# A single-core attention and mixer kernel: even query weights, mixer steps of 5, 5 and 4, and a part of one step's keys on GpSimd's queue

## The chip, the cores and the metric

The kernel runs on one core of a Trainium2 chip. The core has a matrix engine (TensorE, PE in the profile), a vector engine (VectorE, DVE), a scalar engine (ScalarE, ACT), a general one (GpSimd, POOL) and a sync engine (SyncE, SP) that here does nothing but ask for transfers. Sixteen DMA engines move data between the chip's memory and the core's on-chip memory of 128 partitions. The metric is the time of one execution in microseconds (us), lower is better; the time before is the median of 3 runs.

## The reference, cut to what matters

One decode step (one new token for each of 8 sequences) of a block in which attention and a token mixer stand side by side:

```python
# x (8, 1, 512); k_cache, v_cache (8, 8, 8192, 128); wq (512, 4096); wo (4096, 512); F = 1792
xn = layernorm(x)
q = (xn @ wq) as (8 rows, 32 heads, 1, 128)         # 4 query heads share one head of keys
p = softmax(q @ k.T * 128 ** -0.5)                  # over 8192 cached positions
A = (p @ v) as (8, 1, 4096) @ wo
h = layernorm(xn)                                   # (8, 1, 512)
B = gelu(h^T * w1 + b1) @ w2 + b2                   # per batch row: 512 channels, 1792 hidden units
out = x + A + B
```

All is float32. Keys and values are 8 x 8 x 8192 x 128 x 4 bytes = 268 MB each, wq and wo 8.4 MB each; all of it has to be read once.

## The kernel before, in words

The work runs in 32 steps (`duo_step(i)`, i from 0 to 31). A step is one pair of key-value heads of one batch row; its keys and its values are 8 MB each (128 partitions x 64 KB: partition p holds 128 consecutive positions of one of the two heads). They lie in a ring of five slots of 4 MB (`slots`, tile `raw`). A step's keys take two slots and its values two.

In a step, DVE transposes the keys in place, 32 x 32 blocks at a time (L347), in two halves of four instructions; PE multiplies each piece with the queries (L357) into `acc`. After the first half of a step's scores SP may ask for the next step's keys, since the slots that these go to were read by then (`load_next()` at L478). Then comes the maximum (L370), its spread over partitions (L375, L377), the exponential on ACT (L383), a matmul and a transpose that bring the weights into place (L389, L390), and the product with the values of the step before (L398), after whose second half SP asks for the next values (L499). The order in which SP asks is the list `plan`; the order of every engine's instructions is the order of the calls in the code.

Every four steps of a group, `place_duo` (L408 to L428) divides and folds the results. The mixer runs beside it in small steps: `mix(n)` (L455, called at L510 with n = 4) takes the next n of 8 x 14 mixer steps. A mixer step is a GELU on ACT (L443) and a multiplication and an addition on POOL (L444, L445) into `macc`. When a batch row's 14 steps are over, the first mixer step of the next row begins with `mx_end` (PE sums `macc` over partitions, L449, and DVE adds the row to `yrow`, L450) and `mx_begin` (PE L435, POOL L437). With four steps a call, a row of 14 ends inside a call for every second row, and at the start of one for the others.

At the start, wq is loaded in two manners. 448 of its 512 rows go evenly over the partitions, in two loads of 128 x 7168 numbers, into the slots 2 and 3 (`body`, L85, L128). The other 64 rows go into slot 4 (`extra`) by small loads from SP and POOL (L100 to L124), each of which brings a chosen number of rows to chosen DMA engines; tiny loads on POOL (`pass_over`, L111) move the choice of engine on. By the sizes of these loads eight engines receive 4 to 11 rows of 16 KB each and the other eight none. PE multiplies them (L317) in the order of arrival: first and second half of `body`, then `extra`. A DMA of a few rows is spread over the engines row by row; a load over all 128 partitions gives every engine the same.

PE's instructions are themselves fetched by DMA while the program runs: 36 transfers of 16 KB (queue q8 of the profile), which in this trace fall on eight of the sixteen engines in turn, those that get no extra rows of wq.

## Time and profile before

| | us |
|---|---|
| median of 3 runs (1290.19 to 1291.01) | 1290.56 |
| profiled execution | 1292.12 |
| its span, first to last instruction | 1290.4 |
| PE busy with matmuls | 769.5 |
| DVE busy | 685.7 |
| POOL busy | 234.9 |
| ACT busy | 221.2 |
| data moved: 554.39 MB, mean rate | 430 GB/s |
| mean granted TensorE clock | 0.808 of full speed |

The prediction quotes rows of the profile. Rows of DMA queues read: queue, kind, packets, megabytes, share of the time of 16 engines. Rows of the chain read: start (us from the span's start), length, what; the chain goes back from the last instruction to whatever released each piece. Rows of a timeline read: start, busy us, engine, line, operation, output and input tile, shape, and in brackets how long the engine had been idle and what ended that. "L347" is line 347 of the kernel before.

### The profile page before, as it was taken

The numbers are of one execution on the slowest core, as the hardware profiler recorded it, in microseconds if no ns is written. First come the engines' busy times: TensorE is split into PE (matmuls) and PEld (weight loads), VectorE is DVE, ScalarE is ACT, GpSimd is POOL, SyncE is SP. The second block draws the span as 40 slices with busy tenths as digits, with TensorE's granted clock in tenths as the row PEclk, the third lists the DMA queues.
The fourth block names the chain that finished last, engine by engine and source line by source line (L and its number), as shares of the span: only waits on it lengthen the run. The fifth ranks groups of instructions, "written<-read, shape, count | busy, mean of one in ns | idle before, by whom it ended". The sixth has DMA issues, their size and how long they took to land.

```text
span 1290.4 us, 10900 instructions
## 1 busy us (share of the span) xinstructions
PE 769.5 (60%) x4656; PEld 162.6 (13%) x4656; DVE 685.7 (53%) x567; ACT 221.2 (17%) x321; POOL 234.9 (18%) x254
## 2 busy tenths in 40 slices
PE   3665565765556675465565665576456764456676
PEld 1210011110111110011110111111011110011112
DVE  5745544565644465544465554466544565544561
ACT  1030222121221111222121222102222121200000
POOL 3031222022221112222112222102222012200000
PEclk8896777887778877888887787887777877778879
DMA  9999999999999999999999999999999999999998
GB/s 385 434 441 433 433 429 431 440 425 437 435 429 439 429 435 431 433 438 431 434 435 429 431 429 433 427 437 437 429 437 431 431 436 433 435 431 431 441 421 344
DMA packets 12067, 554.39 MB, mean 430 GB/s; under 512 B 1941, under 2 KB 1973, under 8 KB 2369
## 3 DMA queue, kind: packets, MB, share of 16 engines
q1 hardware_dynamic: 11316, 553.08, 99.2%
q8 instruction: 36, 0.59, 0.2%
q0 software_dynamic: 672, 0.61, 0.1%
q14 instruction: 11, 0.09, 0.0%
q10 hardware_dynamic: 32, 0.02, 0.0%
HBM read 553.69 MB, written 0.02 MB: 429 GB/s over the span
## 4 chain that ended last, share of the span: by engine, by line
DMA 71%; DVE 21%; PE 7%; ACT 1%; issue 0%; SPq 0%; POOL 0%; ACTq 0%; DVEq 0%
DMA raw<-in_A_k_cache_dram 60%; DVE raw L347 21%; DMA raw<-in_A_v_cache_dram 7%; PE acc L357 3%; PE acc L398 3%; DMA raw<-in_A_wo_dram 2%; DMA raw<-in_A_wq_dram 1%; PE misc L317 0%; PE misc L422 0%; POOL macc L445 0%; ACT raw L91 0%; PE misc L389 0%; PE misc L449 0%; SPq L187 0%; ACT g L443 0%
## 5 line engine op out<-in xcount | busy, mean ns | idle before, releaser
L347 DVE STREAM_TRANSPOSE raw<-raw 128x2048 f32<-128x2048 f32 x256 | 565.3, 2274 | 215.7 <-DMA raw<-in_A_k_cache_dram 215.7
L357 PE MATMUL acc<-raw,z 128*32 128x512 f32 x2048 | 377.8, 823 | 448.1 <-DVE raw L347 445.7
L398 PE MATMUL acc<-raw,pt 128*32 128x512 f32 x2048 | 242.7, 616 | 7.5 <-DMA raw<-in_A_v_cache_dram 6.9
L444 POOL TENSOR_SCALAR g<-g,pad 128x512 f32<-128x512 f32 x112 | 77.4, 691 | 759.0 <-ACT g L443 759.0
L357 PEld LDWEIGHTS acc<-raw,z 128*32 128x32 f32 x2048 | 47.2, 124 | 763.1 <-DVE raw L347 486.5
L445 POOL TENSOR_TENSOR macc<-macc,g 128x512 f32<-128x512 f32 x112 | 141.6, 1265 | 9.3
L383 ACT ACTIVATE t2k<-acc,nb 128x512 f32<-128x512 f32 x32 | 22.0, 687 | 651.9 <-DVE nb L377 651.9
L443 ACT ACTIVATE g<-hb,pad 128x512 f32<-128x512 f32 x112 | 87.0, 777 | 200.4 <-POOL macc L445 173.5
L390 DVE STREAM_TRANSPOSE pt<-misc 128x512 f32<-128x512 f32 x64 | 45.9, 717 | 139.2 <-PE misc L389 134.7
L398 PEld LDWEIGHTS acc<-raw,pt 128*32 128x32 f32 x2048 | 65.2, 114 | 171.7 <-issue 144.8
L377 DVE CUSTOM_DVE_ANT_0 t2k<-misc,hmask 128x128 f32<-128x128 f32 x32 | 9.3, 292 | 114.5 <-PE misc L375 114.5
L389 PE MATMUL misc<-t2k,send 128*128 128x512 f32 x128 | 63.5, 618 | 2.7 <-ACT t2k L383 2.7
L370 DVE TENSOR_REDUCE mr<-acc 128x1 f32<-128x512 f32 x32 | 22.1, 690 | 51.9 <-PE acc L357 51.9
L406 ACT COPY ob<-acc 128x512 f32<-128x512 f32 x32 | 18.7, 585 | 118.1 <-PE misc L422 55.1
L443 ACT ACT_TABLE_LOAD x28 | 35.9, 1283 | 4.6 <-PE hb L435 4.2
L511 ACT ACT_TABLE_LOAD x28 | 35.9, 1283 | 0.5
L422 PE MATMUL misc<-ob,pick 128*32 128x512 f32 (+2 forms) x72 | 29.0, 546 | 0.7 <-ACT ob L406 0.7
L389 PEld LDWEIGHTS misc<-t2k,send 128*128 128x128 f32 x128 | 21.7, 189 | 44.1 <-issue 41.3
L317 PE MATMUL misc<-raw,ob 128*32 128x512 f32 x88 | 16.9, 890 | 17.2 <-DMA raw<-in_A_wq_dram 17.2
L449 PE MATMUL misc<-macc,bsel 128*8 128x512 f32 x16 | 11.6, 817 | 25.8 <-POOL macc L445 25.8
L450 DVE TENSOR_TENSOR yrow<-misc,yrow 8x512 f32<-8x512 f32 x8 | 5.4, 679 | 30.3 <-PE misc L449 30.3
L437 POOL MEMSET macc<- 128x512 f32 x8 | 4.2, 526 | 89.4 <-PE misc L449 59.7
(91 smaller groups left out, 150.3 us busy)
## 6 DMA issues: line engine op xcount, KB each, us to landing
raw<-in_A_v_cache_dram SPq DMA_DIRECT2D x4, 4096.0 KB
raw<-in_A_k_cache_dram SPq DMA_DIRECT2D x4, 2048.0 KB, 18.2
raw<-in_A_k_cache_dram SPq DMA_DIRECT2D x2, 4096.0 KB
raw<-in_A_wq_dram SPq DMA_DIRECT2D x2, 3584.0 KB, 13.3
raw<-in_A_wo_dram SPq DMA_DIRECT2D x1, 4096.0 KB
raw<-in_A_wo_dram SPq DMA_DIRECT2D x1, 2048.0 KB
raw<-in_A_wo_dram SPq DMA_DIRECT2D x1, 1024.0 KB, 31.1
raw<-in_A_wo_dram SPq DMA_DIRECT2D x1, 512.0 KB
```

Of the source, the lines that this page charges most:

```text
L347: nc.vector.transpose(t, t)
L357: nc.tensor.matmul(SD[i][c * W:(c + 1) * W, :].rearrange("p (t j) -> p t j", j=W), Z[:, q, b, (1 - k) * REP:(1 - k) * REP + W], t[:, c * C ...
L370: nc.vector.tensor_reduce(mr, SD[i], AX.X, ALU.max)
L383: nc.scalar.activation(p, SD.pop(i), AF.Exp, bias=nb, scale=SCALE, accum_out=LD[e][:, o:o + 1])
L389: nc.tensor.matmul(m, send[:, k, :], p, start=True, stop=True)
L390: nc.vector.transpose(PT[k][:, :CH_T * W], m)
L398: nc.tensor.matmul(OD[i][j * W:(j + 1) * W, :].rearrange("p (c d) -> p c d", c=NCH), PT[k][:, t * W:(t + 1) * W], v[:, t], start=(not k an ...
L422: nc.tensor.matmul(mv, pick[:, c, :], ob[:, :n, c * DH:(c + 1) * DH], start=(c == 0), stop=(c == NCH - 1))
L443: nc.scalar.activation(g, hb, AF.Gelu_apprx_tanh, bias=b1t[:, j:j + 1], scale=w1t[:, j:j + 1])
L444: nc.gpsimd.tensor_scalar(g, g, w2t[:, j:j + 1], 1.0, op0=ALU.mult, op1=ALU.mult)
L445: nc.gpsimd.tensor_add(acc, acc, g)
L511: nc.scalar.activation(small.tile([P, 1], F32, name="warm"), nil, AF.Exp)
```

## The change

The 512 rows of wq go evenly over the partitions, 4 rows to each, in two loads of 4 MB, and the query product takes them in that order; the extra rows, the tiny loads at the start, the tiles and copies that served them go. Keys 0 are asked for in two pieces, keys 1 in one. The mixer takes 5, 5 and 4 steps in turn and starts at step 1, so that each row of 14 ends with a call. And of step 14's keys, SP loads partitions 0 to 111 whole and of partitions 112 to 127 the last 1024 of each 8192 numbers; POOL's queue loads the first 7168 of each 8192 there, in four loads of 2, 6, 2 and 6 partitions, ahead of each a tiny load that moves the choice of engine on. By these sizes, each of eight engines receives 2 partitions x 56 KB = 112 KB from POOL's queue, and each of the sixteen 456 KB from SP's.

```diff
-WJ = 14
...
+MIX = (5, 5, 4)
+MID = 14
+EVEN = P - 16
+APART = 7168
+QE = D // P
+QN = HQ * DH
...
-    nc.sync.dma_start(body[:, :half], rows[:, :half])
...
-    load_block(nc.sync, 0, 5, REP, D0, 6)
-    load_steps(nc.sync, W, REP, 3, D0 + 4, 6)
...
-    nc.sync.dma_start(body[:, half:WJ * WB], rows[:, half:])
-    def load_side():
-        pass_over(7)
-        load_block(nc.gpsimd, 60, 2, REP, D0 + 30, 10, 2)
...
+    rows = wq.rearrange("(p e) n -> p (e n)", p=P)
+    for a in range(2):
+        half = slice(a * QE * QN // 2, (a + 1) * QE * QN // 2)
+        nc.sync.dma_start(body[:, half], rows[:, half])
...
-    plan = [(kc, KP, 0, (k,), (k,), x) for k in range(2) for x in halves]
-    plan += [(kc, KP, 1, (2 + k,), (k,), whole) for k in range(2)]
+    plan = [(kc, KP, 0, (k,), (k,), whole) for k in range(2)]
+    plan.append((kc, KP, 1, (2, 3), (0, 1), None))
...
+    def pass_over(n):
+        at = len(passed) * 4
+        passed.append(n)
+        nc.gpsimd.dma_start(junk[:n, at:at + 3:2].unsqueeze(2), wq[:n, 0:3:2].unsqueeze(2))
+
+    def load_uneven(t, rows):
+        nc.sync.dma_start(t[:EVEN], rows[:EVEN])
+        nc.sync.dma_start(t[EVEN:, :, APART:], rows[EVEN:, :, APART:])
+        at = EVEN
+        for skip, n in ((7, 2), (6, 6), (2, 2), (6, 6)):
+            pass_over(skip)
+            nc.gpsimd.dma_start(t[at:at + n, :, :APART], rows[at:at + n, :, :APART])
+            at += n
...
-        if x is None:
+        if to is KP and i == MID:
+            load_uneven(t.rearrange("p (s m) -> p s m", s=2), rows.rearrange("p (s m) -> p s m", s=2))
+        elif x is None:
             nc.sync.dma_start(t, rows)
...
+        for e in range(QE):
+            for h in range(HKV):
+                g = h % NB
+                nc.tensor.matmul(ms[h // NB][g * W:(g + 1) * W, :], lx[:, e, :],
+                                 body[:, e * QN + h * REP * DH:e * QN + (h + 1) * REP * DH],
+                                 start=(e == 0), stop=(e == QE - 1))
+        load_next()
+        load_next()
...
-        mix(4)
+        if i:
+            mix(MIX[(i - 1) % len(MIX)])
```

On SP's queue the start of the program read, before (`raw` is the ring; each row gives the line, the operation, the output and the input, and the shape):

```order
L85 DMA raw<-in_A_wq_dram 128x7168
L100 DMA raw<-in_A_wq_dram 20x1x4096
L105 DMA raw<-in_A_wq_dram 3x8192
L105 DMA raw<-in_A_wq_dram 2x4096
L120 DMA raw<-in_A_wq_dram 3x2x16
L124 DMA raw<-in_A_wq_dram 2x2x16
L128 DMA raw<-in_A_wq_dram 128x7168
L175 DMA raw<-in_A_k_cache_dram 128x4096 x4
L175 DMA raw<-in_A_k_cache_dram 128x8192 x2
L175 DMA raw<-in_A_v_cache_dram 128x8192 x2
```

and with the change:

```order
L83 DMA raw<-in_A_wq_dram 128x8192 x2
L133 DMA raw<-in_A_k_cache_dram 128x8192 x2
L131 DMA raw<-in_A_k_cache_dram 128x16384
L133 DMA raw<-in_A_v_cache_dram 128x8192 x2
L131 DMA raw<-in_A_k_cache_dram 128x16384
```

The five extra loads of wq on SP are gone, and keys 0 and 1 come in three loads instead of six.

On POOL's queue, between the mixer steps that belong to step 12 and those of step 13, the changed program has (`junk` takes the tiny loads):

```order
L370 TENSOR_SCALAR g<-g,pad 128x512
L371 TENSOR_TENSOR macc<-macc,g 128x512
L110 DMA junk<-in_A_wq_dram 7x2x1
L118 DMA raw<-in_A_k_cache_dram 2x2x7168
L110 DMA junk<-in_A_wq_dram 6x2x1
L118 DMA raw<-in_A_k_cache_dram 6x2x7168
L110 DMA junk<-in_A_wq_dram 2x2x1
L118 DMA raw<-in_A_k_cache_dram 2x2x7168
L110 DMA junk<-in_A_wq_dram 6x2x1
L118 DMA raw<-in_A_k_cache_dram 6x2x7168
L363 MEMSET macc 128x512
```

Before, no load stood there: the clearing of `macc` or the next mixer step followed directly.

On PE, the end of the mixer's fifth row stood before inside the call of step 17 (the rows from step 17's second half of values on; L449 is `mx_end`, L435 `mx_begin`):

```order
L398 MATMUL acc<-raw,pt_246 32x512 x16
L389 MATMUL misc<-t2k,send 128x512 x2
L416 MATMUL misc<-lr_1767,ohg 32x4
L422 MATMUL misc<-ob,pick 32x512 x4
L449 MATMUL misc<-macc,bsel 8x512
L435 MATMUL hb<-hn,ident 128x512
L357 MATMUL acc<-raw,z 32x512 x32
```

and stands now at the start of step 16's call, ahead of all mixer steps of that call (L375 is now `mx_end`, L361 `mx_begin`):

```order
L324 MATMUL acc<-raw,pt_165 32x512 x16
L315 MATMUL misc<-t2k,send 128x512 x2
L375 MATMUL misc<-macc,bsel 8x512
L361 MATMUL hb<-hn,ident 128x512
L283 MATMUL acc<-raw,z 32x512 x32
```

In both programs PE has the row's sum right behind the step's other work and ahead of the next step's scores (L357, now L283); what differs is whether mixer steps of the same call stand ahead of it on ACT and POOL: two of them before, none now.

## The prediction

> **What bounds the kernel now.** I read the page first: the queues (its part 3: packets, megabytes, share of the sixteen DMA engines' time) and the chain that ended last (part 4).

> ```profile
> q1 hardware_dynamic: 11316, 553.08, 99.2%
> q8 instruction: 36, 0.59, 0.2%
> DMA raw<-in_A_k_cache_dram 60%; DVE raw L347 21%; DMA raw<-in_A_v_cache_dram 7%; PE acc L357 3%; PE acc L398 3%; DMA raw<-in_A_wo_dram 2%; DMA raw<-in_A_wq_dram 1%; PE misc L317 0%; PE misc L422 0%; POOL macc L445 0%; ACT raw L91 0%; PE misc L389 0%; PE misc L449 0%; SPq L187 0%; ACT g L443 0%
> ```

> SP's queue keeps the sixteen engines busy for 99.2% of the span, at 553.08 MB / (0.992 x 16 x 1290.4 us) = 27.0 GB/s each. The compute lines in the chain are only the way back to a request for keys: while DVE transposes, the queue still holds other loads. Then I read the chain in order of time (start, length, what).

> ```profile
> 8.17 18.68 DMA raw<-in_A_wq_dram
> 67.50 38.13 DMA raw<-in_A_k_cache_dram
> 105.65 8.90 DVE raw L347 x4
> ...
> 183.00 8.90 DVE raw L347 x4
> ...
> 530.72 8.90 DVE raw L347 x4
> 539.66 1.11 PE acc L357 x8
> 540.79 28.48 DMA raw<-in_A_k_cache_dram
> ...
> 729.16 8.81 DVE raw L347 x4
> 738.01 1.11 PE acc L357 x8
> 739.14 23.37 DMA raw<-in_A_k_cache_dram
> 762.60 8.90 DVE raw L347 x4
> ...
> 1228.49 17.67 DVE raw L347 x8
> ```

> DVE's transposes begin as soon as the last of the sixteen engines has delivered a step's keys, so their starts are landing times of the slowest engine. Keys 2 landed at 105.65, keys 4 at 183.00, keys 13 at 530.72, keys 19 at 762.60, keys 31 at 1228.49. From 4 to 13 a step takes 347.72 / 9 = 38.64 us for 16.78 MB: 434 GB/s, 27.1 GB/s for each engine, 19.32 us for a load of 8 MB. From 19 to 31 it takes 465.89 / 12 = 38.82 us, 2.26 us more in all than at the earlier pace. The time is the load of the slowest engine, and which engine that is changes on the way.

> The extra 2.26 us fit the fetches of PE's instructions. There are 36 of 0.59 MB / 36 = 16 KB, one in about 36 us, shared by eight engines: in 466 us 12.9 of them, 1.6 to an engine, so 1.4 us each if the slowest engine is one that fetches. The page's 0.2% (0.15 to 0.25) of 16 x 1290.4 us over 36 gives 0.86 to 1.43 us. I take 1.4. Before 730 us the pace holds no fetch, so there the slowest engine is one of those that carry the uneven rows of wq. Those rows are these (size in KB, median us from issue to landing):

> ```profile
> raw<-in_A_wq_dram SPq DMA_DIRECT2D x2, 3584.0 KB, 13.3
> raw<-in_A_wq_dram SPq DMA_DIRECT2D x1, 320.0 KB
> raw<-in_A_wq_dram POOLq DMA_DIRECT2D x1, 256.0 KB, 13.2
> raw<-in_A_wq_dram POOLq DMA_DIRECT2D x3, 64.0 KB, 23.1
> ```

> wq's even part is 448 KB to an engine, 16.9 us, yet its last byte lands at 8.17 + 18.68 = 26.85. The engines with many extra rows are some 7 us late from then on.

> **The change, part by part.** *Even wq.* By the landing of keys 2 every engine now moves five loads of 512 KB (wq, keys 0 and 1, values 0, keys 2): 5 x 19.32 = 96.6 us. The start loses time besides (stretch, busy times of the engines, PE's clock, DMA share, GB/s):

> ```profile
> 0.00:12.00 12.00, 0.99 (x6) 0.83 (x6) 8.52 (x56) 5.18 (x4) 8.21 (x16) 1.00 0.88 341
> 12.00:24.00 12.00, 5.19 (x28) 1.30 (x28) 9.94 (x50) 0.29 (x1) 1.13 (x2) 1.00 0.98 409
> 24.00:40.00 16.00, 5.96 (x32) 1.44 (x36) 1.93 (x1) 0.00 (x0) 2.80 (x5) 0.72 1.00 422
> ```

> Against 434 GB/s the first 12 us lose 2.6 us and the next 28 us 1.1 us. The first loss stays; the second, where engines wait between pieces of unequal length, may stay or go (0 to 1.1; I keep it whole, since no row shows the start without the pieces). One fetch for the engine that is now slowest, 1.4. Sum: 96.6 + 2.6 + 1.1 + 1.4 = 101.7 instead of 105.65: **-3.9** (-5.0 with the second loss gone). Five extra loads of wq on SP, twelve on POOL, three of the pieces in which keys 0 and 1 were asked for, and the memsets and copies that scattered x go too; they lie beside the load and are worth nothing. PE's matmuls for q fall from 44 to 32; the last 16 of before (two records each) took

> ```profile
> 39.72 6.08 PE L317 MATMUL misc<-raw,ob 128*32 128x512 f32 x32 [7.16 <-DMA raw<-in_A_wq_dram]
> ```

> so the 16 that now stand behind wq's second half, which lands at about 22 us, end by 28; keys 1 are requested then, while keys 0 keep the engines busy until 41.

> *The fetches from then on.* The fetching engines are no longer ahead; they are the slowest all the way. Five fetches fall on the unluckiest of the eight (36 = 4 x 8 + 4), four of them after keys 2: 4 x 1.4 = 5.6 us on top of 29 x 38.64 = 1120.6 us.

> *Step 14's keys.* SP loads 112 rows whole and, of the last 16, only the last 1024 of each 8192 numbers: 7 x 64 KB + 8 KB = 456 KB to an engine instead of 512 KB, -56 KB or **-2.1**. POOL's queue brings 16 x 56 KB = 896 KB, 112 KB to each of eight engines, 4.2 us each. Those eight have no fetches, so by keys 31 they stand at 4.2 against 7.0 and are not last: nothing on the path. The eight POOL issues (four are tiny loads that only move the choice of engines on) cost 0.6 us each,

> ```profile
> 7.93 0.58 POOL L105 DMA_DIRECT2D raw<-in_A_wq_dram  x1
> q0 software_dynamic: 662, 0.61, 4.4%
> ```

> 4.6 us. POOL has nothing else to do then, by its old timeline (start, length, what, idle before):

> ```profile
> 531.35 1.27 POOL L445 TENSOR_TENSOR macc<-macc,g 128x512 f32<-128x512 f32 x1
> ...
> 565.96 0.69 POOL L444 TENSOR_SCALAR g<-g,pad 128x512 f32<-128x512 f32 x1 [33.34 <-ACT g L443]
> ```

> Step 12's mixing is over at 532.6 and step 13's begins 25 us after the request at 540.79. The first of POOL's four data loads waits, as SP's does, for the first half of step 13's scores; queued behind it on POOL are its next mixing steps alone, and for those ACT waits. Without that cover they would slip by at most the 4.6 us. What rows that go through POOL cost the engines shows only at the start (the second row, for 0 to 40 us): 4.4% of 16 x 40 us is 28 us for 0.61 MB in 662 packets, against 22.5 us by size, so large packets run at the common 27 GB/s. That row is the nearest and I take 4.2 us from it. It does not bound the cost from above: those rows were placed apart for the purpose, these 16 lie side by side. From above I take that the 16 rows get only the pace of the two engines that write them today: 896 KB / 54.3 GB/s = 16.9 us, 12.7 us more.

> Keys 2 to 31 then take 1120.6 + 5.6 - 2.1 = 1124.1 us instead of 1122.84: **+1.3**.

> *Mixer steps 5, 5, 4.* Old step 17 closes a batch row inside a call of four, and PE and DVE stand behind POOL:

> ```profile
> 726.57 1.87 PE L449 MATMUL misc<-macc,bsel 128*8 128x512 f32 x2 [7.90 <-POOL macc L445]
> 728.48 0.68 DVE L450 TENSOR_TENSOR yrow<-misc,yrow 8x512 f32<-8x512 f32 x1 [7.64 <-PE misc L449]
> ```

> Keys 18 had landed by about 723.9 (530.72 + 5 x 38.64), the transposes began at 729.16, so keys 19 were requested 5.3 us late (739.14). The usual lead of a request over the last engine is 28.48 - 19.32 = 9.2 us, here 23.37 - 19.32 = 4.05: enough for the slowest engine, not for those ahead, which gave up their lead. Now every batch row closes at the start of a call, with POOL long done. The slowest engine gains nothing at once; that the fetching engines keep their lead is already in the +1.3, which charges them for no idle time. The five-step calls take one step more of ACT and POOL,

> ```profile
> 720.67 0.79 ACT g L443
> ...
> 723.61 0.79 ACT g L443
> ```

> 2.94 us (723.61 - 720.67), and lie where four-step calls left 33.34 us of POOL idle (above): hidden. If that cover went, one step's excess would delay a request by up to 3 us, still within 9.2.

> *The end.* From keys 31 to the end the program is the same: 61.9 us, and 0.

> The sum is -3.9 + 1.3 = **-2.6 us**. The profiled execution took 1292.12 us around its span of 1290.4, the median of the runs is 1290.56; 1290.56 - 2.6 = **1288.0 us**. Apart from the POOL rows the bounds are -3.7 (start's loss gone) and 0 (a fetch at 1.4 with some idle time left to the engines that fetch).

> [...]

> **The rivals.** *The rows crowd.* The pace belongs to the destination, not to the engine: the eight engines queue up before rows that two engines serve today, and everything behind them in their queues waits. They get up to 12.7 us more, of which the 7.0 - 4.2 = 2.8 us by which they were ahead is free: +9.9, so 1288.0 + 9.9 = 1298. It decides once the detour costs an engine more than 7.0 us instead of 4.2, and the result is slower by over 0.2% from 12.1 (7.0 and the 5.1 from 1288.0 to the bound of 1293.1 below). For it: nothing in this trace had two engines write to the same rows' neighbourhood, so nothing excludes it. Against it: the 28 us for 0.61 MB above. [...]

> *The rows come late.* POOL's loads landed up to 23.1 us after issue (above); the last is issued some 5 us after the request, so all may land 28 us after it, as the old load did (28.48). A few us later, and keys 15 are requested later; 9.2 us of lead absorb that, and engines that are ahead lose at most their lead. 1288 to 1291, say 1290.

> *The rows go to other engines.* The tiny loads are to steer the choice; if it stands elsewhere, fetching engines get the 4.2 us: 1288.0 + 4.2 = 1292, just inside no change.

> *More than forecast.* The start's second loss goes and the fetches cost 1.2: -1.1 - 1.0, 1286.

> **How the numbers follow.** A measurement here can tell 0.2%, 2.6 us, from no change: under 1288.0 is faster, over 1293.1 slower. Forecast as summed 0.45, its own range 1286.9 to 1290.5; rows crowd 0.30 (1291 to 1306, a fifth of it within 0.2%); rows late 0.10; other engines 0.08; more than forecast 0.07. The forecast lies on the line between faster and no change and I halve it. Faster: 0.22 + 0.07 = 0.29. No change: 0.23, 0.06 of the crowding, 0.07 of the late rows and 0.05 of the other engines, 0.41. Slower: 0.24, 0.03 and 0.03, 0.30. The range must hold 8 in 10: 1286.5 to 1300.

> **What would show it.** Keys 2 landing at 101.7 and not 105.65; steps of 38.64 us with 1.4 us more where the slowest engine fetched; about 2 us gained at step 14; no DVE wait on PE misc for yrow over 1 us; keys 31 at 1226. Crowding would show as keys 14 or values 13 landing 5 to 15 us behind the pace, and as POOL's packets far slower than 27 GB/s. I am wrong in mechanism if the steps before 14 are slower than 38.8, or if keys 2 land at 105 as before.

## The result, and the profile after

| | us |
|---|---|
| before, median of 5 runs on the same chip | 1291.01 (1290.19 to 1291.21) |
| changed, median of 5 runs | 1331.98 (1330.25 to 1332.48) |
| ratio, with its 95% interval | 1.0315 (1.0302 to 1.0328) |
| span of the changed kernel's profiled execution | 1330.2 |

The change made the kernel 41.0 us slower, where the prediction said 2.6 us faster and left at most 1300 in its range.

The loss can be seen on the page at once. These are the moved gigabytes per second in 40 equal slices of the span, first before (32.3 us a slice) and then of the changed kernel (33.3 us a slice), and behind them the changed kernel's two queues that carry the load:

```profile
GB/s 385 434 441 433 433 429 431 440 425 437 435 429 439 429 435 431 433 438 431 434 435 429 431 429 433 427 437 437 429 437 431 431 436 433 435 431 431 441 421 344
GB/s 407 429 435 434 434 438 427 438 428 435 430 436 432 436 426 436 297 214 288 415 442 436 432 428 434 434 434 432 428 438 430 432 432 440 424 432 439 434 421 333
q1 hardware_dynamic: 10868, 552.75, 98.4%
q0 software_dynamic: 416, 0.94, 0.4%
```

Slices 17 to 19 of the changed kernel, from 532 to 632 us, run at 297, 214 and 288 GB/s; ahead of them and behind them the stream keeps its old pace. It is the stretch in which step 14's keys come. GpSimd's queue (q0) held the engines for 0.4% of 16 x 1330.2 us, some 85 us (74 to 96 by the rounding), for 0.94 MB that would take 35 us at 27.1 GB/s.

The chain of waits in order of time says what stood there (start, length, what):

```profile
101.69 8.90 DVE raw L273 x4
...
529.24 8.90 DVE raw L273 x4
...
540.74 41.39 DMA raw<-in_A_k_cache_dram
...
582.18 10.40 another core or an unknown queue
...
592.66 19.68 another core or an unknown queue
...
612.41 8.90 DVE raw L273 x4
...
622.49 21.96 DMA raw<-in_A_k_cache_dram
...
644.54 8.90 DVE raw L273 x4
```

Keys 2 landed at 101.69 (the prediction said 101.7) and keys 13 at 529.24. These are SP's first request for keys 14 and the last of GpSimd's four (start, length, what):

```profile
539.31 0.34 SPq L113 DMA_DIRECT2D raw<-in_A_k_cache_dram  x1
543.00 0.58 POOL L118 DMA_DIRECT2D raw<-in_A_k_cache_dram  x1
```

Keys 14 had landed whole at 612.41, 73.1 us after SP's request, where the old one took 28.48. The two pieces of "an unknown queue" are waits whose releaser the trace doesn't name; they lie where GpSimd's rows were still coming (the slowest of its four loads took 69.3 us). From keys 13 to keys 15 the changed kernel took 644.54 - 529.24 = 115.3 us, before 2 x 38.64 = 77.3: 38.0 us more, nearly all of the loss.

The stretch in pieces (stretch, busy times of the engines with their instructions, PE's clock, DMA share, GB/s):

```profile
546.00:580.00 34.00, 17.89 (x91) 4.51 (x91) 6.24 (x11) 5.64 (x8) 6.37 (x7) 0.71 0.96 199
584.00:592.00 8.00, 0.00 (x0) 0.00 (x0) 0.00 (x0) 0.56 (x2) 1.19 (x1) 0.50 0.98 143
594.00:608.00 14.00, 0.00 (x0) 0.00 (x0) 0.00 (x0) 0.00 (x0) 0.00 (x0) 0.50 1.00 277
614.00:622.00 8.00, 5.45 (x32) 0.75 (x32) 8.00 (x5) 0.00 (x0) 0.00 (x0) 0.72 0.21 90
626.00:640.00 14.00, 13.48 (x91) 2.98 (x84) 5.07 (x5) 1.27 (x3) 0.00 (x0) 0.78 1.04 449
```

The last two columns are what matter. From 546 to 580 all sixteen engines are busy (share 0.96) and move 199 GB/s: none waits for work, each piece takes twice as long (the median of those of 64 KB 4.85 us, where it is 2.42 from 626 to 640). It gets worse from 584 to 592 (143 GB/s), when the rest of the keys and values 13, which SP asks for next, are on the queues together. From 614 to 622 the share falls to 0.21: now there is nothing to move, because keys 15 are asked for only after keys 14 have come, at 622.49.

GpSimd's loads in that stretch (size, median us from issue to landing):

```profile
raw<-in_A_k_cache_dram POOLq DMA_DIRECT2D x2, 336.0 KB, 55.4
raw<-in_A_k_cache_dram POOLq DMA_DIRECT2D x2, 112.0 KB, 35.6
```

The prediction expected them to cost the engines 4.2 us each and to land with the rest.

### The profile page after: what moved, and what is told of

It reads as the page before. It is cut to its first block, busy times and chain, and to the rows that moved or that the text cites. A ratio compares the mean times of both kernels' runs of the same rounds, so it can differ in the third digit from the quotient of the medians.

```text
span 1330.2 us, 10766 instructions
## 1 busy us (share of the span) xinstructions
PE 747.7 (56%) x4630; PEld 161.3 (12%) x4630; DVE 677.8 (51%) x509; ACT 206.9 (16%) x311; POOL 230.5 (17%) x249
## 4 chain that ended last, share of the span: by engine, by line
DMA 72%; DVE 21%; PE 4%; another core or an unknown queue 2%; issue 0%; SPq 0%; POOL 0%; DVEq 0%
DMA raw<-in_A_k_cache_dram 66%; DVE raw L273 21%; PE acc L283 3%; DMA raw<-in_A_wo_dram 2%; DMA raw<-in_A_v_cache_dram 2%; DMA raw<-in_A_wq_dram 2%; PE acc L324 1%; PE misc L243 0%; SPq L145 0%; POOL raw L118 0%; PE misc L301 0%; POOL junk L110 0%; DVEq L273 0%; PE hb L460 0%
## 5 line engine op out<-in xcount | busy, mean ns | idle before, releaser
L283 PE MATMUL acc<-raw,z 128*32 128x512 f32 x2048 | 369.4, 806 | 521.3 <-DVE raw L273 508.9
L283 PEld LDWEIGHTS acc<-raw,z 128*32 128x32 f32 x2048 | 47.1, 123 | 829.7 <-DVE raw L273 492.9
L350 DVE TENSOR_TENSOR t2k<-misc,keep 32x512 f32<-32x512 f32 (+2 forms) x9 | 5.7, 629 | 22.6 <-PE misc L348 22.6
L243 PE MATMUL misc<-raw,ob 128*32 128x512 f32 x64 | 9.3, 732 | 12.3 <-DMA raw<-in_A_wq_dram 12.3
L262 PE MATMUL misc<-qt,rep 128*64 128x32 f32 x64 | 3.0, 243 | 13.4 <-DVE qt L255 13.4
```

Source lines behind the costliest of these rows:

```text
L283: nc.tensor.matmul(SD[i][c * W:(c + 1) * W, :].rearrange("p (t j) -> p t j", j=W), Z[:, q, b, (1 - k) * REP:(1 - k) * REP + W], t[:, c * C ...
```

## The experiments

The theories, as far as they were formed ahead of the first runs: A, the loss belongs to the place that is written, and a load over 128 partitions is dealt to the engines so that no two of them write to the same group of partitions, while a load of another shape is not (which engine writes which partitions is an assumption of the author's; no trace shows it); B, it belongs to GpSimd's queue; C, to the rows of memory that are read.

The diffs are cut to the lines that matter. They stand against the changed kernel for e1_even, e2_split, e3_ways and e5_rows, against e2_split for e8_leave, against e1_even for e7_even4, e9_stagger, e10_pieces and e11_pad, and against the kernel before for e6_mix and e12_shift.

**The change without its keys part (e1_even).**

```diff
-MID = 14
+MID = -1
```

> The change without its keys part: even query weights and mixer steps of 5, 5 and 4 stay, step 14's keys come in one load of 128 partitions from SP. If the whole loss sits in step 14's keys, the time falls back by the 38.0 us that keys 13 to keys 15 took longer there (115.3 against 77.28 us), to 1331.98 - 38 = 1294, or lower by what the rows were to save on the fetching engines: the prediction's sum without the -2.1 gives 1290.1. So 1290 to 1294. If even weights or the mixer's steps had a part in the loss, more than 1296.

Measured: 1294.56 us (1294.41 to 1295.08), ratio to before 1.0025 (1.0016 to 1.0034). The chain:

```profile
101.72 8.90 DVE raw L273 x4
...
529.35 8.90 DVE raw L273 x4
...
567.98 8.90 DVE raw L273 x4
...
606.81 8.90 DVE raw L273 x4
...
646.72 8.90 DVE raw L273 x4
```

Keys 13 to 15 take 606.81 - 529.35 = 77.46 us. So the keys part costs 1331.98 - 1294.56 = 37.4 us. But 1294.56 is also just over the upper edge of what was expected (1290 to 1294): 4.5 us above the sum without the rows (1290.1). That is a second question, taken up below.

**SP alone, 112 partitions and then 16 (e2_split).**

```diff
-        nc.sync.dma_start(t[EVEN:, :, APART:], rows[EVEN:, :, APART:])
-        at = EVEN
-        for skip, n in ((7, 2), (6, 6), (2, 2), (6, 6)):
-            pass_over(skip)
-            nc.gpsimd.dma_start(t[at:at + n, :, :APART], rows[at:at + n, :, :APART])
-            at += n
+        nc.sync.dma_start(t[EVEN:], rows[EVEN:])
```

> The changed kernel with nothing on GpSimd's queue: SP loads 112 partitions of step 14's keys whole and then the 16 others whole. Theory A, the place: a load over 128 partitions is dealt to the engines so that each writes groups of partitions of its own, and in a load of another shape several engines meet in the same group and all go at the pace of the fullest. Then the 112 rows run at half pace (7 rows of 64 KB for an engine at 4.83 us, 33.8 us, against 16.9), the 16 consecutive rows, four to a group, at a quarter (9.7 us): step 14's keys take 43.5 us instead of 19.3, +24, some 1316 us, and the DMA rate in that stretch is near 220 GB/s. Theory B, the queue: GpSimd's loads slow the engines; then there is no loss here, 1290 to 1294. Theory C, the memory side: engines that read 448 KB apart instead of 512 KB meet in the memory; then the 112 rows run at half pace and the 16 others do not, +17, 1309.

Measured: 1325.24 us (one run), 30.7 above e1_even, with nothing of the keys on GpSimd's queue. Two stretches of it, the 112 rows and then the 16, and the landing of keys 14:

```profile
546.00:572.00 26.00, 17.80 (x91) 4.64 (x91) 6.35 (x11) 3.42 (x5) 1.29 (x3) 0.85 0.94 220
576.00:590.00 14.00, 0.00 (x0) 0.00 (x0) 0.00 (x0) 3.82 (x5) 5.98 (x7) 0.50 1.11 127
...
598.63 8.90 DVE raw L268 x4
```

220 GB/s for the 112 rows as expected, and 127 for the second stretch. That one holds more than the 16 rows: 127 GB/s for 14 us are 1.78 MB, the rows 1.05 MB, so the first of values 13 were slow beside them. Theory B falls as the cause of the whole: the loss is there without GpSimd. The loss is 7 us more than the 24 worked out, and all of it is there when keys 14 land (598.63 against 567.98 in e1_even); where these 7 us come from isn't shown.

**The 112 rows alone (e8_leave).** The last 16 partitions of step 14's keys are not loaded at all.

```diff
-        nc.sync.dma_start(t[EVEN:], rows[EVEN:])
```

> Of step 14's keys SP loads partitions 0 to 111 whole, and the 16 others are left out (they keep what lay in the slot, so the output is not the reference's; 1 MB less is moved). Theory A (place): the 112 rows take 7 x 4.83 = 33.8 us instead of 19.3 for the whole, so keys 15 land 14.5 us later than with an even load, which took 77.46 us from keys 13 to keys 15: about 92 us, and the time is 1294.6 + 14.5 = 1309. If the half pace came from the 16 rows, or from GpSimd's loads, these 112 rows take 16.9 us and the time is 1292. What is left of the 38 us then belongs to the 16 rows and to their late landing.

Measured: 1311.67 us (one run), 17.1 above e1_even, although 1 MB less is moved. The 112 rows and, behind them, an ordinary stretch:

```profile
546.00:574.00 28.00, 18.42 (x95) 4.69 (x91) 6.28 (x11) 4.20 (x6) 3.28 (x5) 0.80 0.96 223
...
590.00:620.00 30.00, 18.21 (x125) 3.92 (x122) 15.39 (x11) 4.35 (x7) 3.90 (x4) 0.90 1.01 435
```

Half pace (223 against 435 GB/s) with all engines busy, for a load that leaves the last 16 partitions out. So of the 37.4 us, 17.1 come from the 112 rows that SP still loads, and 20.3 from the other 16 rows and from when they land.

**Other shapes (e3_ways).** No uneven load; the keys of steps 5, 11, 17 and 23 (the `else`) come in other shapes.

```diff
+        if i == 5:
+            by = rows.rearrange("(e r) m -> e r m", r=8)
+            nc.sync.dma_start(t[:EVEN], by[:, :7])
+            nc.sync.dma_start(t[EVEN:], by[:, 7])
+        elif i == 11:
+            for r in range(8):
+                nc.sync.dma_start(t[16 * r:16 * r + 16], rows[16 * r:16 * r + 16])
+        elif i == 17:
+            for r in range(8):
+                nc.sync.dma_start(t[r::8], rows[r::8])
+        else:
+            for r in range(0, P, 32):
+                for o in range(4):
+                    nc.sync.dma_start(t[r + o:r + 32:4], rows[r + o:r + 32:4])
```

> Even weights, mixer steps of 5, 5 and 4, no uneven load; the keys of four steps come from SP in other shapes. Step 5: 112 partitions side by side, filled from rows of memory that lie as in an even load (blocks of 8 rows, 7 of each), and then 16 (the rows land in the wrong order, so the output is not the reference's). Step 11: eight loads of 16 partitions side by side. Step 17: eight loads of 16 partitions eight apart. Step 23: sixteen loads of 8 partitions four apart. Theory A (place), with groups of four partitions and those 32 further on sharing one: step 5 takes 43.5 us as before (+24), step 11 meets four to a group, 8 x 9.7 = 77 us (+58), step 17 two to a group, 38.6 us (+19), step 23 one to a group, full pace, but on eight engines alone, 38.6 us (+19) with the other eight idle; some 1292 + 120 = 1412 us. Theory C (memory side): step 5 at full pace but for nothing, 19.3 us; steps 11 and 17 read rows side by side and eight apart from memory, and whichever of them is slow is so by where it reads.

Measured: 1448.54 us (one run). A stretch of each of the four steps, in their order, and an ordinary one:

```profile
206.00:220.00 14.00, 7.61 (x41) 2.00 (x40) 2.41 (x5) 4.20 (x6) 3.58 (x5) 0.81 0.90 234
460.00:500.00 40.00, 13.68 (x73) 3.62 (x73) 2.41 (x5) 8.02 (x11) 10.29 (x11) 0.63 0.99 140
738.00:766.00 28.00, 0.00 (x0) 0.00 (x0) 0.00 (x0) 0.00 (x0) 0.00 (x0) 0.50 1.01 213
1014.00:1046.00 32.00, 0.00 (x0) 0.00 (x0) 0.00 (x0) 0.00 (x0) 0.00 (x0) 0.50 0.51 219
1120.00:1160.00 40.00, 21.67 (x141) 4.41 (x141) 21.19 (x15) 7.24 (x10) 7.81 (x8) 0.83 0.98 422
```

The groups by which the expectation adds up theory A's times are an assumption of the author's, and no run shows them by themselves. Its times make 217 GB/s for steps 17 and 23 (8.39 MB in 38.6 us), which the trace bears out (213 and 219), and 109 for step 11 (8.39 MB in 77 us), where the trace has 140: there the measurement decides. Why it is better than that sum is open; SP asked for step 11's eight loads within 18 us of 448.40, so an engine may have begun the next load, at other partitions, while others still wrote the one before.

The time is 36 us above the 1412 expected. Two stretches show what the sum had left out, and so do DVE's transposes of step 16's keys in their two halves:

```profile
780.00:796.00 16.00, 13.02 (x93) 2.78 (x97) 9.61 (x7) 0.78 (x2) 0.00 (x0) 0.75 0.00 1
1050.00:1068.00 18.00, 11.79 (x89) 2.70 (x93) 9.88 (x7) 0.78 (x2) 0.00 (x0) 0.79 0.00 1
...
719.27 8.89 DVE L280 STREAM_TRANSPOSE raw<-raw 128x2048 f32<-128x2048 f32 x4 [7.83 <-DMA raw<-in_A_k_cache_dram]
779.73 8.89 DVE L280 STREAM_TRANSPOSE raw<-raw 128x2048 f32<-128x2048 f32 x4 [51.57 <-DMA raw<-in_A_k_cache_dram]
```

After the slow keys of steps 17 and 23 there was nothing to move (1 GB/s) for 16 and 18 us. In step 16 (and so in step 22) the second half of the transposes stood still until the next step's keys had landed, 51.57 us, where in the steps around it both halves run without a wait; the values that follow are asked for only behind that half. From keys 16 to keys 18 it took 42.8 us more than in e1_even and from keys 22 to keys 24 38.5, where 19 each were expected; step 11 cost 47.7 us instead of 58, and step 5 25.4 instead of 24. Why the second half waits isn't shown; only the two steps whose next keys go to partitions with gaps have it, and in the changed kernel no step does.

**The 16 rows once more, after an even load (e5_rows).**

```diff
-        nc.sync.dma_start(t[:EVEN], rows[:EVEN])
-        nc.sync.dma_start(t[EVEN:, :, APART:], rows[EVEN:, :, APART:])
+        nc.sync.dma_start(t, rows)
```

> SP loads step 14's keys in one load of 128 partitions, and GpSimd's queue loads the 16 rows' 896 KB once more into the same place, after the first load has landed (896 KB more are moved than in the change). It shows what these rows cost beside an even stream (values 14, and then keys 15). Theory A: the four groups of partitions 112 to 127 get 224 KB each on top of their share, at 27 GB/s 8.3 us, in which every engine is held up, and the step's scores wait for the rows: keys 15 are late by 8 us and by what the rows land later than that. Theory B (the queue alone is slow): the rows take over 30 us and the values beside them run at half pace, although each engine is given only 112 KB. If rows through that queue cost only their size, 4.2 us, the time is below 1300.

Measured: 1323.63 us (one run), 29.1 above e1_even. The even load, then values 13 (values 14 in the expectation are these) with the rows, the rows almost alone, and nothing; then the larger two of GpSimd's loads (size, median us from issue to landing):

```profile
546.00:572.00 26.00, 16.62 (x95) 4.09 (x91) 6.26 (x11) 3.42 (x5) 3.28 (x6) 0.83 0.98 422
...
584.00:592.00 8.00, 0.00 (x0) 0.00 (x0) 0.00 (x0) 2.26 (x3) 2.05 (x3) 0.50 1.05 140
592.00:602.00 10.00, 0.00 (x0) 0.00 (x0) 0.00 (x0) 0.00 (x0) 0.00 (x0) 0.50 0.30 60
602.00:612.00 10.00, 4.93 (x24) 0.59 (x24) 8.26 (x4) 0.00 (x0) 0.00 (x0) 0.57 0.00 0
...
raw<-in_A_k_cache_dram POOLq DMA_DIRECT2D x2, 336.0 KB, 31.3
```

The even load over 128 partitions runs at 422 GB/s. Beside the rows everything falls to 140 with all engines busy: 896 KB for 16 partitions hold up sixteen engines, not the eight that carry them. Then the stream is empty for 10 us, as in the changed kernel at 614, since keys 15 are asked for only behind the first half of step 14's scores: late keys cost twice, as load and as an empty stream behind them. So the 16 rows are dear in every way tried: 13.6 us by SP in one piece (1325.24 - 1311.67), 20.3 in the change, and 29.1 where they come after the rest. GpSimd's queue isn't needed for the loss; but its larger loads took 31.3 us from issue to landing here, and over 30 us was the sign put down for theory B. So a slow queue isn't excluded as a part of the cost of these 16 rows, and how much of the 20.3 is its own can't be told from these runs, since the rows there also land later.

**What the even weights and the mixer's steps cost (e7_even4, e6_mix).** e1_even was 3.4 us above the runs of before beside it (1291.2). Mixer steps of 4 in the even kernel, and of 5, 5 and 4 in the kernel before:

```diff
-        if i:
-            mix(MIX[(i - 1) % len(MIX)])
+        mix(4)
```

> Even query weights alone: mixer steps of 4 from step 0 on, step 14's keys in one load. With e1_even (1294.56) it parts the 3.4 us that even weights and mixer steps cost together. If the mixer's steps are worth nothing either way, 1294.5; if ends of rows inside a call cost lead that is needed at the end, 1295 to 1297; if the loss of e1_even is that of the mixer's steps, 1290 to 1291.

Measured: 1294.62 us, ratio 1.0024 (1.0014 to 1.0035).

```diff
-        mix(4)
+        if i:
+            mix(MIX[(i - 1) % len(MIX)])
```

> The kernel before with the mixer's steps of 5, 5 and 4 alone. The prediction let the wait of step 17 cost the slowest engine nothing at once, and the engines ahead their lead. If that lead counts at the end, 1289 to 1290.5; if it does not, the time of before, 1291 within 0.1%.

Measured: 1291.34 us against 1291.49, ratio 1.0001 (0.9991 to 1.001). The mixer's steps are worth nothing in either kernel: 1294.62 against 1294.56, 1291.34 against 1291.49. The lead that the wait of step 17 takes away isn't needed at the end.

**The kernel before once more (c0_before).** No edit.

> The kernel before once more, for a second trace of it on the chip that runs the others. Its first trace was of an execution of 1292.12 us, 1.1 us above the median of its runs (1291.01), and the prediction's landing times rest on it. If that trace was of an ordinary execution, the span is 1290.4 and keys 2, 13 and 31 land at 105.65, 530.72 and 1228.49 again; if not, about 1289 and the steps from 13 on are shorter.

Measured: one run of 1290.54 us, span 1288.8. Keys 2 and keys 31:

```profile
105.03 8.90 DVE raw L347 x4
...
1226.81 17.68 DVE raw L347 x8
```

The first trace of before was of a long execution: its span was 1290.4, and it took 1122.84 us from keys 2 to keys 31, here 1121.78.

**Why the steps of the even kernel are longer (e9_stagger, e10_pieces).** From keys 2 to keys 13 e1_even takes 529.35 - 101.72 = 427.63 us; less one fetch of 1.4 and over 11 steps that is 38.75, where the kernel before has 38.64. The two first theories:

```diff
+    for n, p, c in ((12, 0, 0), (8, 0, 1), (4, 96, 0)):
+        nc.sync.dma_start(slots[p:p + 8 * n:8, 4, c * QN:(c + 1) * QN], wq[:n])
```

> e1_even with three small loads more behind wq, of 12, 8 and 4 rows of 16 KB into a slot that is free then: engines get 3, 2, 1 or 0 of them, 0.6 us each, so that they no longer run in step (their data is not used). It asks why e1_even's steps without a fetch take 38.70 to 38.82 us where the kernel before takes 38.64. Theory D, in step: sixteen engines that begin their 64 KB pieces at the same moment slow each other a little, and engines that are apart do not; then the steps take 38.64, which saves 29 x 0.11 = 3.2 us, against up to 1.8 us more at the start: 1292.5 to 1294. Theory E, something else in even weights (the pieces in which keys 0 and 1 come, or the engines that end last): the steps stay at 38.75 and the time is 1294.5 to 1296.5.

Measured: 1297.87 us, ratio 1.005 (1.0036 to 1.0063). From its chain:

```profile
105.98 8.90 DVE raw L275 x4
144.75 8.90 DVE raw L275 x4
183.44 8.90 DVE raw L275 x4
```

The steps stay at 38.77 and 38.69: that the engines run in step isn't it. Keys 2 landed at 105.98 instead of 101.72, 4.3 us later for loads that should cost 1.8; they too are of 12, 8 and 4 partitions.

```diff
-    plan = [(kc, KP, 0, (k,), (k,), whole) for k in range(2)]
-    plan.append((kc, KP, 1, (2, 3), (0, 1), None))
+    plan = [(kc, KP, 0, (k,), (k,), x) for k in range(2) for x in halves]
+    plan += [(kc, KP, 1, (2 + k,), (k,), whole) for k in range(2)]
```

> e1_even with keys 0 and 1 in the pieces of the kernel before, four loads of 128 x 4096 and two of 128 x 8192 instead of two and one. Theory D (in step): every engine still gets the same, steps stay at 38.75 and the time at 1294.5. If the pieces set the pace of the whole stream, steps of 38.64 and 1291.5.

Measured: 1295.04 us, ratio 1.003 (1.0019 to 1.004). The pieces aren't it either.

**Where the ring begins (e11_pad, e12_shift).** What was left (theory F) is one line of the diff: the tile `pad` lies ahead of the ring, and with the extra rows it lost the columns that the tiny loads wrote to. It shrank from 96 to 74 numbers a partition, and the ring moved from byte 16896 to byte 16832.

```diff
-    pad = place.tile([P, 3 * NF + W], F32, name="pad")
+    pad = place.tile([P, 96], F32, name="pad")
```

> e1_even with the tile ahead of the ring as wide as in the kernel before, 96 numbers to a partition and not 74, so that the ring begins where it did (byte 16896 of each partition, a multiple of 256, and not 16832). Theory F, the start of the ring: every piece that is written into a ring off that boundary takes a little longer, and that is why the steps without a fetch take 38.75 us instead of 38.64 whatever the pieces (e10_pieces) and the offsets of the engines (e9_stagger). Then they take 38.64 here: 29 steps give back 3.1 us, wq and the first keys some 0.2 more, and the time is 1294.56 - 3.3 = 1291.3, that of the kernel before. If the ring's start is not it, 1294.5.

Measured: 1291.56 us, ratio 1.0001 (0.9992 to 1.001). From its chain:

```profile
101.57 8.90 DVE raw L273 x4
...
566.64 8.90 DVE raw L273 x4
...
605.35 8.90 DVE raw L273 x4
...
645.46 8.90 DVE raw L273 x4
...
1227.86 17.68 DVE raw L273 x8
```

From keys 2 to keys 14, less one fetch, a step is (566.64 - 101.57 - 1.4) / 12 = 38.64 us. The even kernel is back at the time of before: 3.0 us less (1294.56 - 1291.56; against the runs of before beside each, 3.4 and 0.0) for 88 bytes a partition that nobody uses.

```diff
-PAD = 384
+PAD = 424
```

> The kernel before with the tile ahead of the ring wider by 40 bytes to a partition, so that the ring begins at byte 16960, as far past a multiple of 256 as 64 bytes; nothing else is changed. Theory F: steps of 38.75 instead of 38.64 us, some 3 us more, 1294. If the ring's start does not count, 1291.2.

Measured: 1293.85 us against 1291.56, ratio 1.0021 (1.0012 to 1.0031). A shift by 64 bytes in the kernel before costs 2.3 us. Theory F holds from both sides. The traces' records of single pieces point the same way: between 140 and 520 us the median piece of 64 KB takes 2.418 us in the trace of before, with the ring at byte 16896, and 2.420 in that of the changed kernel, with the ring at 16832. The runs show 0.2% (3.0 of 1291.56 and 2.3 of 1291.56 us) for a start 64 bytes below and one 64 bytes above byte 16896; whether it is the multiple of 256 that the expectation names, or something else about that place, isn't shown.

So the 41.0 us, by medians: 37.4 from step 14's keys (17.1 the 112 rows on SP, 20.3 the 16 rows), 3.0 from the ring's start, and what is left, about half a microsecond either way, from even weights and mixer steps together.

## Why the prediction was wrong

**What bounds the kernel: right.** The time was the stream's before and is the stream's after, but for some 8 us from 614 on, in which little was left to move (90 GB/s) and the first half of step 14's transposes and scores stood between keys 14 and the request for keys 15.

**The start, -3.9: right in the sum, in part by luck.** Keys 2 at 101.69 in the changed kernel, 101.7 forecast. Against the second trace of before (105.03) it is -3.3. The start of the changed kernel, in the prediction's three stretches:

```profile
0.00:12.00 12.00, 0.61 (x4) 0.55 (x4) 7.94 (x39) 1.58 (x2) 3.09 (x10) 1.00 0.88 352
12.00:24.00 12.00, 6.58 (x44) 1.75 (x48) 2.47 (x8) 0.29 (x1) 0.00 (x0) 1.00 1.02 437
24.00:40.00 16.00, 4.62 (x44) 2.48 (x36) 7.23 (x4) 1.17 (x2) 0.00 (x0) 0.73 0.99 426
```

Against 434 GB/s the first 12 us lose 2.3 us (2.6 forecast) and the next 28 some 0.2 (1.1 forecast). By these parts keys 2 should have landed at 100.5; what the other 1.2 us are isn't shown.

**The fetches, 1.4 each on the slowest engine: right, and the sum with them.** In e11_pad, which is the change without rows and shift, one step in seven is longer: 645.46 - 605.35 = 40.11 beside 605.35 - 566.64 = 38.71, 1.4 more. From keys 2 to keys 31 it took 1227.86 - 101.57 = 1126.29 us; the prediction's 1120.6 + 5.6 is 1126.2. This balance alone would have left the kernel where it was: its span is 1289.7, against 1289.9 by the prediction's terms without the rows (1290.4 - 3.9 + 3.4) and 1288.8 in the second trace of before.

**Step 14's keys, -2.1 on SP: the step that failed, and in its sign.** It took bytes for an engine as the only price ("456 KB to an engine instead of 512 KB") and the common pace for the 112 rows. In these runs that pace is that of loads over all 128 partitions (434 GB/s). The 112 rows ran at 220 GB/s and cost 17.1 us more, where 2.1 less were put down. The ends of this term were not looked for at all; doubt was spent on GpSimd's rows alone.

**GpSimd's rows, 4.2 us on eight engines: wrong.** The 16 rows, with the eighth of them that SP loads, cost 20.3. The row it was taken from (0.61 MB for 28 us of engine time at the start) was of rows that had been given places of their own, as the prediction itself said. Its bound from above, 16.9 us, let the rows slow only the engines that carry them and that write there today, two by the author's estimate, which no trace shows; e5_rows shows all sixteen held up (140 GB/s at a share of 1.05). How much of the 20.3 is the place and how much GpSimd's queue stays open. The issue slots on POOL (0.6 us each, nothing queued behind them that matters) were as forecast: POOL's next work came 25 us later.

**The landing.** "All may land 28 us after it" became 73.1, and a lead of 9.2 us doesn't absorb that: from 614 to 622 the stream stood nearly empty. In the trace GpSimd's 32 pieces of 28 KB begin from 544.8 to 606.6 us, one by one among SP's pieces.

**The rivals.** "The rows crowd" named the mechanism that the shapes of e3_ways speak for, the pace of the destination, at 0.30, but put it in the wrong load and on eight engines, and so ended at 1306. The groups of partitions in theory A's sums, with which e2_split, e3_ways and e5_rows went on from this rival, are shown by no run; what the runs showed is a pace for each shape, 220 to 234 GB/s for 112 partitions side by side, 140 for 16 side by side, 213 for 16 eight apart and 219 for 8 four apart. "The rows come late" was right that they would be late. No case had both, and none was long enough.

**Even weights: a term that was missing.** "The memsets and copies that scattered x go too; ... worth nothing" was true of them. But with them a tile became shorter, the ring moved by 64 bytes, and that cost 3.0 us. No step of the prediction had asked what else the removed code had held in place.

**The mixer's steps: right.** Nothing gained at once, and nothing later: 1.0001 (0.9991 to 1.001).

**The base.** The profiled execution of before took 1292.12 us, 0.6 to 1.1 above the medians of before here (1291.01 to 1291.56), and the second one (1290.54) 0.5 to 1.0 below them; their spans are 1.6 us apart (1290.4 and 1288.8). Landing times from one execution are uncertain by about 1 us. Beside the other errors it is small, but it is a good part of a gain of 2.6.

## What to carry to other kernels

Ask of each load not only how many bytes an engine gets, but which partitions the sixteen engines write at one time: the shapes tried here that weren't over all 128 ran at 140 to 234 GB/s instead of 434, and a load of 16 partitions also slowed what came with it. Before work is moved between engines, look at the place that it is written to as well; the kernel before does it with rows of wq, whose place is free. And when code is removed, look at where the big tiles begin afterwards: here 64 bytes cost 3.0 us, more than the 2.6 that the whole change was to win.

## What the runs showed that was not expected

- Eight loads of 16 partitions side by side, one behind the other, ran at 140 GB/s, where the expectation's sum makes 109 (8.39 MB in 77 us).
- 112 rows at half pace kept all sixteen engines busy (share 0.96 at 223 GB/s); no engine ran ahead of another: in the changed kernel's trace the 44 pieces of 64 KB that begin from 549.0 to 561.8 us take 4.73 to 5.20 us each, where an even one takes 2.42. That the fullest place sets the pace for all fits these numbers, and no run shows it by itself.
- Three small loads, 24 rows of 16 KB in all, put the landing of keys 2 off by 4.3 us (105.98 against 101.72), 2.5 more than the bytes of the fullest engine.
- The start of the ring, at byte 16832 or 16960 instead of 16896, is worth 0.2% of a stream of 553 MB.
